# Attention and an exact-GELU feed-forward layer on one core: the first batch's masks, loads and order rewritten

## The chip, the core and the metric

The kernel runs on one core of a Trainium2 chip. A core has TensorE (PE, matmuls into PSUM), VectorE (DVE), ScalarE (ACT), GpSimd (POOL) and SyncE (SP), each with its own instruction stream, and 16 DMA engines that serve the queues of all of them. The metric is the device time of one execution in microseconds (us); lower is better. Before the change the median of 10 runs was 339.84 us (338.58 to 342.14).

## What is computed

Eight batches of eight heads of causal attention over 576 positions of 64 dimensions, with a decay bias from a running sum of s, and then a feed-forward layer over the 4608 tokens (512 to 2048 to 512) with the exact GELU.

```python
scores = scale * np.matmul(q, k.transpose(0, 1, 3, 2))
cum = np.cumsum(np.maximum(s, 0.0), axis=-1)
bias = -(cum[:, :, :, None] - cum[:, :, None, :])
scores = np.where(causal, -1000000000.0, scores + np.minimum(bias, 0.0))
attn = softmax(scores)
x = np.matmul(attn, v)            # to (tokens, heads * dims)
h = x @ w_in
out = (0.5 * h * (1.0 + erf(h / sqrt(2)))) @ w_out
```

The kernel uses that the bias splits into a factor per key position, exp(cum), that can be multiplied into v and into the denominator; numbers that would not allow it send it into a general branch at its end, which these inputs do not take.

## The kernel before

The work goes in chunks of 512 tokens, nine in all; chunk c is the feed-forward work on tokens whose attention was done beforehand, and the attention of batch b = c + 1 is placed between the matmuls of chunk c by a table written by hand. Batch 0 has no chunk to hide in: it is a prologue. The instructions of each engine stand in the order in which the code is written.

A batch's attention has these steps, each a function. `load_qk(b, i, g)` (line 85) loads q (i = 0) or k (i = 1) of one group g of four heads by four DMAs on GpSimd's queue that cast fp32 to bf16 on the way; `load_v` and `load_w` load v (fp32), w_in (`which` 0) and w_out (1), the weights in four pieces each, cast as well. `tr_qk` (197) transposes q or k of a group on VectorE. `sc_item` (348) computes the scores of one group and one unit: unit 0 covers the first two key blocks of 128, unit 1 the other three; four heads take 32 rows of the array each and run beside one another, and ScalarE takes the exp of two heads at a time into P. `mk_item` (359) multiplies the diagonal blocks of P by a 0/1 triangle on VectorE. `weights` (234) makes the running sum `cum` on VectorE, transposes it on TensorE and takes its exp on ScalarE into `wb`; `scale_v` multiplies v by it, `den_col` puts it beside v as a 65th column. `av_item` (422) multiplies P with that for one block `it` of 128 queries; VectorE then takes the reciprocal and scales. `to_xT` (402) transposes the result for the feed-forward layer, by TensorE and a VectorE copy, or by DMA. `absmax` and `square_v` feed a check of ranges.

Chunk c then has layer 1, `l1_item` (449), w_in times xT and the GELU on ScalarE, eight items of two row blocks; and layer 2, `l2_item` (469), which sums 16 matmuls for each block of 128 tokens in one PSUM buffer of two, and evicts it (in chunk 0 by ScalarE) to `o_sb`. `groups` runs layer 2 in steps and calls what the table `side` has for each step. In chunk 0 layer 1 runs twice over 256 tokens, so that it can begin when two blocks of batch 0 are there; `late` names the rest of batch 0's AV between its items.

The prologue has functions of its own. `sc_first` (372) computes scores two heads at a time. It does not use `mk_item`: two more matmuls per piece (line 393) add -30000 above the diagonal by a product of the identity (`ident_bf`) and a mask (`neg_bf`), which `masks` (192) makes on VectorE. k of both groups comes as fp32 into `k0_st`, group 0 on ScalarE's queue, group 1 on SyncE's behind s, and ScalarE casts each (`cast_k0`, 136); q comes through GpSimd. `filler(n)` (416) runs n matmuls of zeros on TensorE, whose results nobody reads. The order is written from line 505 on: the table load for exp, the cast of group 0, 16 fillers, `weights`, the cast of group 1, 4 fillers, all of GpSimd's loads, and then the transposes, scores and AV.

GpSimd's queue before the change: q of group 0, the two triangular selects that make `ident` and `uptri`, q of group 1, v and w_in mixed, two pieces of w_out, q and k of batch 1's group 0, a piece of w_out, q, a piece of w_out, k, v of batch 1.

Of the kernel before, what the change touches and what calls it, by code (L numbers as in the profile page):

```python
# [19 lines left out]
def kernel(  # L20
# [10 lines left out]
    nc = tc.nc  # L31
    fp32 = mybir.dt.float32
# [89 lines left out]
    k0_st = work.tile([128, HG, S * 2], fp32, tag="rawv", bufs=2, name="k0_st")  # L122

    def load_k0(g, eng):

        for h in range(4):
            eng.dma_start(
                out=k0_st[h * 32 : h * 32 + 32, g, :].rearrange("p (t c) -> p t c", c=2 * D),
                in_=bass.AP(
                    tensor=k.tensor,  # L130
                    offset=k.offset + (4 * g + h) * S * D,
                    ap=[[2 * D, 32], [64 * D, SB], [1, 2 * D]],
                ),
            )

    def cast_k0(g):
        nc.scalar.activation(raws[0, "qk"][:, 1, g, :], k0_st[:, g, :], func=AF.Copy)
# [3 lines left out]
    load_k0(0, nc.scalar)  # L141
    load_k0(1, nc.sync)
# [15 lines left out]
    nc.vector.memset(zero, 0.0)  # L158
    ident = const.tile([128, 128], fp32, name="ident")
# [8 lines left out]
    load_qk(0, 0, 1)  # L168
# [21 lines left out]
    neg_bf = const.tile([128, 128], bf16, name="neg_bf")  # L190
# [43 lines left out]
    def weights():  # L234
# [3 lines left out]
        nc.vector.tensor_scalar(cum, s_pos, s_pos[:, 287:288], None, op0=ALU.subtract)  # L238
        t_ps = ps.tile([128, ST, BH], fp32, tag="av", bufs=2, name="t_ps")
# [132 lines left out]
    def sc_first(g, u):  # L372

        if u == 0:
            P_of[0, g] = work.tile([128, 4, PW], bf16, tag="P", bufs=2, name="P")
# [3 lines left out]
        for h2 in range(2):  # L379
            s_ps = ps.tile([128, 2, 512], fp32, tag="sc", bufs=2, name="sc_ps")  # L380
            for jt, i0, n, off in UNITS[u]:
                for e in range(2):
                    for h in range(2):
# [5 lines left out]
                            start=(e == 0), stop=False, tile_position=(h0, 0),  # L389
                        )  # L390
                m = min(n, 128)
                for h in range(2):
                    nc.tensor.matmul(  # L393
                        s_ps[:, h, off : off + m], lhsT=ident_bf, rhs=neg_bf[:, :m],
                        start=False, stop=True,
                    )
# [109 lines left out]
    cast_k0(0)  # L506
    filler(16)
    weights()
    cast_k0(1)
    filler(4)  # L510
# [31 lines left out]
    filler(2)  # L542
    to_xT(0, 0, True)
    filler(1)
    to_xT(0, 1, True)
    gelu_set()
# [7 lines left out]
    for c in range(NCH):  # L554
# [4 lines left out]
        if c == 0:  # L559

            late = [
                [(scale_v, 0, 2), (av, 0, 0, 2)], [(av, 0, 1, 2)],
                [(scale_v, 0, 3), (av, 0, 0, 3)], [(av, 0, 1, 3), (to_xT, 0, 2, True)],
                [(scale_v, 0, 4), (av, 0, 0, 4)], [(av, 0, 1, 4), (to_xT, 0, 3, True)],
                [], [(to_xT, 0, 4, True)],
            ]
            for half in range(2):
                for f2 in range(FT // 2):
                    l1_item(0, f2, half * 256, half * 256 + 256)
                    for f, *a in late[f2] if half == 0 else []:  # L570
                        f(*a)
            for g in range(HG):
                absmax(0, g)
# [21 lines left out]
        if b < B:  # L595
# [5 lines left out]
            if c == 0:  # L601
                for st in range(3):
                    square_v(0, st)
                side = [[] for _ in range(16)]
                side[3] = [(sc, b, 0, 0)]
                side[5] = [(sc, b, 0, 1), (mk, b, 0, 0), (square_v, 0, 3), (square_v, 0, 4)]
                side[6] = [(tr_qk, b, 0, 1), (tr_qk, b, 1, 1)]
                side[9] = [(mk, b, 0, 1), (scale_v, b, 0)]
                side[10] = [(sc, b, 1, 0), (scale_v, b, 1)]
                side[11] = [(av, b, 0, 0), (scale_v, b, 2)]  # L610
                side[12] = [(av, b, 0, 1), (sc, b, 1, 1), (mk, b, 1, 0), (av, b, 0, 2), (scale_v, b, 3)]
                side[13] = [(av, b, 1, 0), (av, b, 0, 3), (scale_v, b, 4)]
                side[14] = [(av, b, 1, 1), (mk, b, 1, 1)]
                side[15] = [
                    (av, b, 1, 2, True), (av, b, 1, 3, True), (to_xT, b, 2, True), (to_xT, b, 3, True)
                ]
# [8 lines left out]
            else:  # L625

                side = [[] for _ in range(16)]
                sc_at = (2, 5, 7, 10) if b < 4 else (2, 5, 8, 11)
# [5 lines left out]
                for at, (g, u) in zip((5, 8, 11, 13 if b < 4 else 14), [(0, 0), (1, 0), (0, 1), (1, 1)]):  # L634
                    side[at].append((mk, b, g, u))
# [165 lines left out]
```

## Time and profile before

| | |
|---|---|
| median of 10 runs | 339.84 us |
| the profiled execution, its own time | 340.57 us |
| its span, first to last instruction | 338.8 us |
| TensorE busy, mean granted clock | 318.6 us (94%), 0.959 |
| VectorE, ScalarE, GpSimd busy | 189.3, 187.5, 87.2 us |
| prologue: to the first layer-1 matmul | 35.20 us, granted clock 0.66 |
| layer 1 of chunk 0 | 35.20 to 52.67 us |
| layer 2 of chunk 0 with batch 1's attention | to 76.7 us |

In the tables of the profile a busy time is the time in which an engine had an instruction under way, and "x" counts instructions. In the timeline the columns are the start, the length, the engine, the line of the kernel, the operation, what it writes and reads, and in brackets the idle time of that engine just before and what ended it. "PEclk" is the share of its full clock that TensorE was granted. A DMA's row gives what it carries, the queue that issued it, the number of issues and the time from issue to landing.

### The profile page before, as it was taken

To read this page: it belongs to the slowest core of one execution; us is meant where nothing else is said; L and a number is where in the kernel's file an instruction comes from. 1 tells how busy PE (TensorE), PEld (TensorE's weight loads), DVE (VectorE), ACT (ScalarE), POOL (GpSimd) and SP (SyncE) were. 2 spreads that over 40 slices of the span, in tenths; PEclk is the share of its full clock that TensorE was granted. 3 is DMA by queue.
4 is the path that set the end of the run, shared out by engine and by line. 5 is a ranking of instruction groups with operands and counts; after the bars stand their busy time and mean duration, and the time that the engine had idled before them with its cause. 6 is when DMAs were issued, how large, how long until landed. Compare 5 with 4: busy or idle time off the path is not lost.

```text
span 338.8 us, 6343 instructions
## 1 busy us (share of the span) xinstructions
PE 318.6 (94%) x2549; PEld 158.4 (47%) x2549; DVE 189.3 (56%) x393; ACT 187.5 (55%) x249; POOL 87.2 (26%) x144
## 2 busy tenths in 40 slices
PE   7599899789998999899999999999999999999992
PEld 2135785344444544454445444545454545444440
DVE  5502672499946794678458744965596542150020
ACT  1445358655877466746576657656857494204400
POOL 7844739103782019000900190000000000000000
PEclk9655999999999999999999999999999999999997
DMA  9999989628999709670998199701310221110011
GB/s 185 218 224 180 152 187 95 111 80 174 139 213 180 185 11 144 123 185 12 134 132 186 26 155 142 172 8 64 93 33 8 77 83 31 41 62 32 3 65 68
DMA packets 92376, 37.35 MB, mean 110 GB/s; under 512 B 80691, under 2 KB 87091, under 8 KB 92339
## 3 DMA queue, kind: packets, MB, share of 16 engines
q0 software_dynamic: 41440, 15.41, 38.6%
q1 hardware_dynamic: 49680, 20.87, 25.5%
q10 hardware_dynamic: 1216, 0.59, 0.7%
q8 instruction: 22, 0.36, 0.4%
q14 instruction: 18, 0.12, 0.1%
HBM read 36.85 MB, written 9.44 MB: 137 GB/s over the span
## 4 chain that ended last, share of the span: by engine, by line
PE 87%; DVE 6%; DMA 2%; ACT 1%; issue 1%; POOL 0%; ACTq 0%; DVEq 0%; POOLq 0%
PE h_ps L460 36%; PE o_ps L476 34%; PE av L428 5%; PE sc_ps L340 5%; PE sc_ps L385 3%; DMA raw_qk<-in_q_dram 2%; PE sc_ps L393 2%; DVE x L438 2%; PE f_ps L420 1%; DVE P L363 1%; DVE vv L222 1%; ACT sq L214 1%; PE xt_ps L411 1%; ACT P L355 1%; DVE o_sb L486 1%
## 5 line engine op out<-in xcount | busy, mean ns | idle before, releaser
L476 PE MATMUL o_ps<-w_out_r,gT 128*128 128x512 bf16 x576 | 135.3, 380 | 1.9 <-ACT o_sb L484 1.9
L460 PE MATMUL h_ps<-xT,w_in_r 128*128 128x512 bf16 (+1 forms) x640 | 132.6, 358 | 1.3 <-DVE xT L414 1.0
L465 ACT ACTIVATE gT<-h_ps 128x1024 bf16<-128x1024 f32 (+1 forms) x80 | 74.8, 938 | 73.9 <-PE h_ps L460 73.5
L460 PEld LDWEIGHTS <-w_in_r 128*128 128x128 bf16 x640 | 59.9, 98 | 55.2 <-issue 2.2
L476 PEld LDWEIGHTS <-gT 128*128 128x128 bf16 x576 | 52.1, 98 | 59.6 <-issue 5.2
L355 ACT ACTIVATE P<-sc_ps 128x1024 bf16<-128x1024 f32 x56 | 54.3, 1021 | 35.0 <-PE sc_ps L340 35.0
L91 POOL DMA_DIRECT2D raw_qk<-in_q_dram x64 | 38.6, 616 | 100.8 <-DVE amx L206 76.7
L486 DVE COPY o_sb<-o_ps 128x512 f32<-128x512 f32 x32 | 22.1, 692 | 59.2 <-PE o_ps L476 59.2
L437 DVE RECIPROCAL rc<-av 128x4 f32<-128x4 f32 (+1 forms) x80 | 14.3, 178 | 59.4 <-PE av L428 59.2
L206 DVE TENSOR_REDUCE amx<-raw_qk 128x2 f32<-128x2304 bf16 x16 | 40.2, 2536 | 0.0
L428 PEld LDWEIGHTS <-P 128*128 128x128 bf16 x576 | 28.2, 99 | 20.9 <-DVE P L363 3.9
L91 POOL DMA_DIRECT2D raw_qk<-in_k_dram x56 | 33.7, 620 | 10.7 <-DMA w_out_r<-in_moe_w_out_dram 5.3
L428 PE MATMUL av<-vv,P 128*128 128x65 bf16 x576 | 32.2, 196 | 3.7 <-DVE P L363 2.3
L438 DVE TENSOR_TENSOR x<-av,rc 128x256 bf16<-128x256 f32 (+1 forms) x80 | 33.8, 423 | 2.8
L363 DVE TENSOR_TENSOR P<-P,tri_bf 128x1024 bf16<-128x1024 bf16 x28 | 19.2, 686 | 13.0 <-ACT P L355 13.0
L222 DVE TENSOR_TENSOR vv<-raw_v,wb 128x512 bf16<-128x512 f32 (+1 forms) x40 | 25.8, 688 | 0.0
L199 DVE STREAM_TRANSPOSE qkT<-raw_qk 128x576 f32<-128x576 f32 x32 | 23.0, 754 | 3.8 <-DMA raw_qk<-in_q_dram 3.8
L214 ACT ACTIVATE sq<-raw_v 128x512 bf16<-128x512 f32 (+1 forms) x40 | 24.6, 624 | 0.0
L340 PE MATMUL sc_ps<-qkT 32*128 32x256 bf16 (+2 forms) x560 | 18.3, 250 | 0.0
L340 PEld LDWEIGHTS <-qkT 32*128 32x128 bf16 x560 | 11.8, 92 | 12.3 <-issue 11.2
L398 ACT ACTIVATE P<-sc_ps 128x1024 bf16<-128x1024 f32 x8 | 8.2, 1023 | 12.7 <-PE sc_ps L393 12.7
L385 PE MATMUL sc_ps<-qkT 32*128 32x256 bf16 (+2 forms) x80 | 10.4, 357 | 4.2 <-DVE qkT L199 4.2
(75 smaller groups left out, 109.7 us busy)
## 6 DMA issues: line engine op xcount, KB each, us to landing
out_dram<-o_sb SPq DMA_DIRECT2D x36, 256.0 KB, 2.4
raw_v<-in_v_dram SPq DMA_DIRECT2D x24, 256.0 KB, 4.0
raw_qk<-in_q_dram POOLq DMA_DIRECT2D x64, 72.0 KB, 3.9
raw_qk<-in_k_dram POOLq DMA_DIRECT2D x56, 72.0 KB, 4.1
raw_v<-in_v_dram POOLq DMA_DIRECT2D x8, 256.0 KB, 5.5
w_in_r<-in_moe_w_in_dram POOLq DMA_DIRECT2D x4, 512.0 KB, 9.2
w_out_r<-in_moe_w_out_dram POOLq DMA_DIRECT2D x4, 512.0 KB, 11.1
raw_v<-in_v_dram SPq DMA_DIRECT2D x6, 128.0 KB, 4.2
```

The lines of the kernel that those rows point to most:

```text
L91: nc.gpsimd.dma_start(out=raws[b, "qk"][h * 32 : h * 32 + 32, i, g, :].rearrange("p (t c) -> p t c", c=2 * D), in_=bass.AP(tensor=src.tens ...
L206: nc.vector.tensor_reduce(amx[:, b * HG + g], raws[b, "qk"][:, :, g, :], axis=AX, op=ALU.max, apply_absolute_value=True,)
L214: nc.scalar.activation(sq[:n_st], raws[b, "v"][:n_st, st].rearrange("p h d -> p (h d)"), func=AF.Square, accum_out=sumv[:n_st, b, st : st ...
L222: nc.vector.tensor_tensor(vv[b % 2][:n_st, st, :, 0:D], raws[b, "v"][:n_st, st, :, :], w.unsqueeze(2).to_broadcast([n_st, H, D]), op=MULT,)
L340: nc.tensor.matmul(s_ps[h // 2][:, h % 2, off : off + n], lhsT=qk[r, 1, g, jt * 128 : jt * 128 + 128, e], rhs=qk[r, 0, g, i0 : i0 + n, e], ...
L355: nc.scalar.activation(P[:, 2 * h2 : 2 * h2 + 2, o : o + 512], s_ps[h2], func=AF.Exp, scale=scale)
L428: nc.tensor.matmul(o_ps[:, h, :], lhsT=P[:, h, off : off + 128], rhs=vv[b % 2][:, jt, 4 * g + h, :], start=(i == 0), stop=(i == len(BLK[it ...
L438: nc.vector.tensor_tensor(x_of[b, it][:n, g * 256 : g * 256 + 256].rearrange("p (h d) -> p h d", d=D), o_ps[:n, :, 0:D], rc[:n].unsqueeze( ...
L460: nc.tensor.matmul(h_ps[:, i, :], lhsT=w_in_r[:, ko, ft * 128 : (ft + 1) * 128], rhs=xT[:, ko, c * NB + n0 : c * NB + n1], start=(ko == 0) ...
L465: nc.scalar.activation(gT_of[c][:, f2 * 2 : f2 * 2 + 2, n0:n1], h_ps, func=AF.Gelu)
L476: nc.tensor.matmul(y_of[c, sub], lhsT=gT[:, ft, sub * 128 : (sub + 1) * 128], rhs=w_out_r[:, ft, :], start=(ft == 0), stop=(ft == FT - 1),)
L486: nc.vector.tensor_copy(o_sb, y_of[c, sub])
```

## The change

Batch 0's masks move from TensorE to VectorE: `sc_first` loses the mask matmuls, and `mk_item` is called for batch 0 too. k of group 0 alone comes as fp32, on SyncE's queue behind s, and is cast in two halves, one by ScalarE and one by VectorE; q and k of group 1 both come through GpSimd, issued right behind q of group 0 and ahead of the selects for `ident` and `uptri`. TensorE gets 26 fillers in a row at the start. `weights` splits: its running sum stays early (`cum_sum`), its transposes and exps come after the first scores. The loads of w_out go ahead of all of batch 1. The prologue interleaves scores, products, AV and transposes in a new order; `late` places batch 0's remaining AV over both halves of layer 1, with three of its squares. In chunk 0's layer 2 each block of 128 tokens runs by itself, where before the first two ran as a pair, with a new table `side`; and in later batches up to 3 the last unit's scores and products come one step earlier.

```diff
-    def load_k0(g, eng):
+    def load_k0(eng):
...
-    def cast_k0(g):
-        nc.scalar.activation(raws[0, "qk"][:, 1, g, :], k0_st[:, g, :], func=AF.Copy)
+    def cast_k0():
+        nc.scalar.activation(raws[0, "qk"][:, 1, 0, :S], k0_st[:, :S], func=AF.Copy)
+        nc.vector.tensor_copy(raws[0, "qk"][:, 1, 0, S:], k0_st[:, S:])
...
-    load_k0(0, nc.scalar)
-    load_k0(1, nc.sync)
+    load_k0(nc.sync)
     load_qk(0, 0, 0)
...
     nc.vector.memset(zero, 0.0)
+    load_qk(0, 0, 1)
+    load_qk(0, 1, 1)
     ident = const.tile([128, 128], fp32, name="ident")
...
-    load_qk(0, 0, 1)
...
     def masks():
-        nc.vector.tensor_scalar(neg_bf, uptri, 30000.0, -30000.0, op0=MULT, op1=ALU.add)
...
-                            start=(e == 0), stop=False, tile_position=(h0, 0),
+                            start=(e == 0), stop=(e == 1), tile_position=(h0, 0),
                         )
-                m = min(n, 128)
-                for h in range(2):
-                    nc.tensor.matmul(
-                        s_ps[:, h, off : off + m], lhsT=ident_bf, rhs=neg_bf[:, :m],
-                        start=False, stop=True,
-                    )
             filler(1)
...
     exp_set()
-    cast_k0(0)
-    filler(16)
-    weights()
-    cast_k0(1)
-    filler(4)
+    filler(26)
...
-    load_w(1, 0)
-    load_w(1, 1)
-    for i in range(2):
-        load_qk(1, i, 0)
-    for i in range(2):
-        load_w(1, 2 + i)
-        load_qk(1, i, 1)
+    for i in range(4):
+        load_w(1, i)
+    load_qks(1)
     load_v(1, nc.gpsimd)
+    cum_sum()
+    cast_k0()
     tr_qk(0, 0, 0)
-    masks()
     tr_qk(0, 1, 0)
     sc_first(0, 0)
-    sc_first(0, 1)
-    den_col(0)
+    weights()
+    filler(2)
     tr_qk(0, 0, 1)
     tr_qk(0, 1, 1)
+    masks()
     sc_first(1, 0)
+    mk_item(0, 0, 0)
+    den_col(0)
     for st in range(2):
         scale_v(0, st)
+    sc_first(0, 1)
     av_item(0, 0, 0)
+    mk_item(0, 1, 0)
+    av_item(0, 1, 0)
+    sc_first(1, 1, (0,))
     av_item(0, 0, 1)
-    sc_first(1, 1)
-    av_item(0, 1, 0)
+    sc_first(1, 1, (1,))
+    to_xT(0, 0, True)
     av_item(0, 1, 1)
     filler(2)
-    to_xT(0, 0, True)
-    filler(1)
     to_xT(0, 1, True)
+    mk_item(0, 0, 1)
+    scale_v(0, 2)
+    mk_item(0, 1, 1)
     gelu_set()
...
-                side[3] = [(sc, b, 0, 0)]
+                side[4] = [(sc, b, 0, 0)]
...
-                groups(c, (0, 1), side[:8])
-                groups(c, (2,), side[8:12])
-                groups(c, (3,), side[12:])
+                for sub in range(4):
+                    groups(c, (sub,), side[4 * sub : 4 * sub + 4])
...
-                sc_at = (2, 5, 7, 10) if b < 4 else (2, 5, 8, 11)
+                sc_at = (2, 5, 7, 9) if b < 4 else (2, 5, 8, 11)
```

On TensorE, at the end of the first half unit of scores (`sc_ps` is the score buffer, `qkT` the transposed q and k, `f_ps<-zero` a filler), before:

```order
L385 LDWEIGHTS qkT_105
L385 MATMUL sc_ps<-qkT_105 128x256
L393 LDWEIGHTS ident_bf
L393 MATMUL sc_ps<-neg_bf,ident_bf 128x128
L393 LDWEIGHTS ident_bf
L393 MATMUL sc_ps<-neg_bf,ident_bf 128x128
L420 LDWEIGHTS zero
L420 MATMUL f_ps<-zero 128x512
L385 LDWEIGHTS qkT_105
L385 MATMUL sc_ps<-qkT_105 128x256
```

The same place after:

```order
L385 LDWEIGHTS qkT_105
L385 MATMUL sc_ps<-qkT_105 128x256
L414 LDWEIGHTS zero
L414 MATMUL f_ps<-zero 128x512
L385 LDWEIGHTS qkT_105
L385 MATMUL sc_ps<-qkT_105 128x256
```

The two mask matmuls and their weight loads are gone from each piece; score, filler and the next half follow one another.

On VectorE, from the running sum of s to the products of batch 0, before:

```order
L238 TENSOR_SCALAR cum<-s_pos 64x576
L199 STREAM_TRANSPOSE qkT_105<-raw_qk 128x9x2x32
L193 TENSOR_SCALAR neg_bf<-uptri 128x128
L194 CAST ident_bf<-ident 128x128
L195 CAST tri_bf<-uptri 128x128
L199 STREAM_TRANSPOSE qkT_105<-raw_qk 128x9x2x32
L230 COPY vv_103<-wb 128x40
L199 STREAM_TRANSPOSE qkT_105<-raw_qk 128x9x2x32 x2
L222 TENSOR_TENSOR vv_103<-raw_v,wb 128x8x64 x2
```

The same stretch after (`k_st` is the fp32 k, `P` the exps, `tri_bf` the 0/1 triangle):

```order
L236 TENSOR_SCALAR cum<-s_pos 64x576
L138 CAST raw_qk<-k_st 128x576
L197 STREAM_TRANSPOSE qkT_105<-raw_qk 128x9x2x32 x4
L192 CAST ident_bf<-ident 128x128
L193 CAST tri_bf<-uptri 128x128
L363 TENSOR_TENSOR P<-P,tri_bf 128x4x2x128
L228 COPY vv_103<-wb 128x40
L220 TENSOR_TENSOR vv_103<-raw_v,wb 128x8x64 x2
L431 RECIPROCAL rc<-av 128x4
L432 TENSOR_TENSOR x<-av,rc 128x256
L363 TENSOR_TENSOR P<-P,tri_bf 128x4x2x128
```

Half of k's cast stands ahead of the transposes, the masks' operations behind all four of them, and the products of P stand between the work for AV.

On GpSimd, the loads from the last two pieces of w_in on (`raw_qk` here is batch 1's), before:

```order
L155 DMA w_in_r<-in_moe_w_in_dram 128x4x512 x2
L155 DMA w_out_r<-in_moe_w_out_dram 128x4x512 x2
L91 DMA raw_qk<-in_q_dram 32x9x128 x4
L91 DMA raw_qk<-in_k_dram 32x9x128 x4
L155 DMA w_out_r<-in_moe_w_out_dram 128x4x512
L91 DMA raw_qk<-in_q_dram 32x9x128 x4
L155 DMA w_out_r<-in_moe_w_out_dram 128x4x512
L91 DMA raw_qk<-in_k_dram 32x9x128 x4
L113 DMA raw_v<-in_v_dram 128x8x64 x4
```

The same loads after:

```order
L155 DMA w_in_r<-in_moe_w_in_dram 128x4x512 x2
L155 DMA w_out_r<-in_moe_w_out_dram 128x4x512 x4
L91 DMA raw_qk<-in_q_dram 32x9x128 x4
L91 DMA raw_qk<-in_k_dram 32x9x128 x4
L91 DMA raw_qk<-in_q_dram 32x9x128 x4
L91 DMA raw_qk<-in_k_dram 32x9x128 x4
L113 DMA raw_v<-in_v_dram 128x8x64 x4
```

The four pieces of w_out stand together, and batch 1's q and k follow them, where half of these loads stood between the pieces before.

More of the change, by code (lines that the diff above doesn't have):

```diff
@@ L378, in sc_first @@
         qk = qkT[0]
-        for h2 in range(2):
+        for h2 in halves:
             s_ps = ps.tile([128, 2, 512], fp32, tag="sc", bufs=2, name="sc_ps")
@@ L569 @@
                     l1_item(0, f2, half * 256, half * 256 + 256)
-                    for f, *a in late[f2] if half == 0 else []:
+                    for f, *a in late[8 * half + f2]:
                         f(*a)
+                    if half == 0 and f2 in (3, 5, 7):
+                        square_v(0, f2 // 2 - 1)
             for g in range(HG):
```

45 lines of the change are left out of this document (22 added, 23 removed).

## The prediction

> **What bounds the kernel now.** I read the page first, then the windows by stage, then the timeline of the first 75 us and the DMA answers. From the page, the load on the engines over the span:
>
> ```profile
> PE   7599899789998999899999999999999999999992
> PEclk9655999999999999999999999999999999999997
> DMA  9999989628999709670998199701310221110011
> ```
>
> TensorE is busy almost everywhere, so the end moves with TensorE. Two things stand out near the start: the granted clock is at 0.5 to 0.6 in slices 2 to 4 (each slice is 8.5 us), and the DMA engines are full for 50 us. The windows of the prologue and of chunk 0's layer 1 (columns: length, busy time of each engine, granted clock, DMA share, GB/s), and finer ones around the clock's changes (length, PE busy, clock, DMA):
>
> ```profile
> 0.00:35.20 35.20, 28.60 (x188) 11.17 (x189) 12.83 (x35) 13.34 (x14) 22.20 (x38) 0.66 1.18 196
> 35.20:52.67 17.47, 16.51 (x188) 14.62 (x188) 12.78 (x23) 8.96 (x15) 9.12 (x14) 1.00 0.94 161
> ...
> 8.00:8.50 0.50, 0.31 (x2) 1.00 1.57 209
> 10.50:11.00 0.50, 0.00 (x0) 0.88 1.28 334
> 34.50:35.00 0.50, 0.18 (x2) 0.73 0.45 29
> ```
>
> The prologue costs 35.2 us and almost all of batch 0's scores run at half clock. Matmuls stop at 8.31. A window's mean of 0.88 puts the drop to 0.5 at 10.88; 0.73 puts the return at 34.77. Next, the timeline at the places that set the prologue's length:
>
> ```profile
> 1.21 5.02 PE L420 MATMUL f_ps<-zero 128*128 128x512 bf16 x16 [1.21 <-DVE zero L158]
> 9.03 1.16 ACT L137 ACTIVATE raw_qk<-k_st 128x1152 bf16<-128x1152 f32 x1 [5.06 <-DMA k_st<-in_k_dram]
> 10.10 0.36 ACT L245 ACTIVATE wb<-t_ps 128x256 bf16<-128x256 f32 x1
> 10.53 0.78 DVE L199 STREAM_TRANSPOSE qkT<-raw_qk 128x576 f32<-128x576 f32 x1 [3.83 <-DMA raw_qk<-in_q_dram]
> 11.73 0.77 DVE L199 STREAM_TRANSPOSE qkT<-raw_qk 128x576 f32<-128x576 f32 x1
> 12.55 0.61 PE L385 MATMUL sc_ps<-qkT 32*128 32x256 bf16 x4 [4.24 <-DVE qkT L199]
> 14.71 0.61 PE L385 MATMUL sc_ps<-qkT 32*128 32x256 bf16 x4
> 15.25 0.39 PE L393 MATMUL sc_ps<-neg_bf,ident_bf 128*128 128x128 bf16 x2
> 16.30 0.63 PE L420 MATMUL f_ps<-zero 128*128 128x512 bf16 x1
> 16.55 1.02 ACT L398 ACTIVATE P<-sc_ps 128x1024 bf16<-128x1024 f32 x1 [1.14 <-PE sc_ps L393]
> 16.87 0.61 PE L385 MATMUL sc_ps<-qkT 32*128 32x256 bf16 x4
> 35.20 1.03 PE L460 MATMUL h_ps<-xT,w_in_r 128*128 128x256 bf16 x8 [0.52 <-DVE xT L414]
> ```
>
> q's landing releases the first transpose at 10.53, the scores start at 12.55, and then one half unit takes 2.16 us from 14.71 to 16.87: two pieces of scores at 0.54 (14.71 to 15.25), two pairs of mask matmuls at 0.33 (to 15.58), a filler at 0.43. ScalarE needs 1.02 of that and idles. So up to 35 us the bound is q's landing, then TensorE at half clock.
>
> **The first score.** How the first transfers share the engines, 0 to 20 us, and the landing of the last of SyncE's k transfers (issued 3.22) and of the last q transfer of group 0 (issued 3.2):
>
> ```profile
> q10 hardware_dynamic: 1216, 0.59, 11.1%
> ...
> k_st<-in_k_dram SPq DMA_DIRECT2D x1, 144.0 KB, 6.7
> ...
> raw_qk<-in_q_dram POOLq DMA_DIRECT2D x1, 72.0 KB, 7.2
> ```
>
> k lands at 9.9 on SyncE's queue and q at 10.4. ScalarE's four k transfers take 11.1% of 20 us, 2.2 us of all 16 engines, and they leave this contest: the second group of k comes by GpSimd behind both groups of q. I take k at 7.7 and q at 8.3; they cannot be later than 9.9 and 10.5 unless the second group gets in front, and 6.6 is my lower end for k, if SyncE's queue gains one and a half times what ScalarE's gives up. The cast is halved over two engines, 1.16 / 2 = 0.6, and hidden under q's landing. VectorE then transposes q and k (0.75 each, the rows at 10.53 and 11.73); the masks' three operations no longer stand between. First score: 8.4 + 1.5 = 9.9 in place of 12.55. Of the 26 fillers the first 16 end at 6.2, and ten more at 0.22 at 8.4: TensorE is idle for 1.6 us in place of 4.2.
>
> **The pace of the scores.** Rows at full clock (three timelines: four fillers; four heads' scores and the exps; AV, VectorE's share of it, the mask product, and a gap in layer 2):
>
> ```profile
> 7.27 1.04 PE L420 MATMUL f_ps<-zero 128*128 128x512 bf16 x4
> 37.19 0.41 PE L428 MATMUL av<-vv,P 128*128 128x65 bf16 x8
> 37.63 0.18 DVE L437 RECIPROCAL rc<-av 128x4 f32<-128x4 f32 x1 [0.47 <-PE av L428]
> 37.84 0.42 DVE L438 TENSOR_TENSOR x<-av,rc 128x256 bf16<-128x256 f32 x1
> 56.22 0.63 PE L340 MATMUL sc_ps<-qkT 32*128 32x256 bf16 x16
> 56.89 1.94 ACT L355 ACTIVATE P<-sc_ps 128x1024 bf16<-128x1024 f32 x2 [0.16 <-PE sc_ps L340]
> 61.51 0.69 DVE L363 TENSOR_TENSOR P<-P,tri_bf 128x1024 bf16<-128x1024 bf16 x1 [0.61 <-ACT P L355]
> 62.12 0.28 DVE L368 TENSOR_TENSOR P<-P,tri_bf 128x256 bf16<-128x256 bf16 x1
> 63.22 2.75 PE L476 MATMUL o_ps<-w_out_r,gT 128*128 128x512 bf16 x12 [1.88 <-ACT o_sb L484]
> 34.72 0.42 DVE L414 COPY xT<-xt_ps 128x512 bf16<-128x512 bf16 x1 [0.43 <-PE xt_ps L411]
> ```
>
> The change takes 40 mask matmuls off TensorE. A half of unit 0 at full clock: scores between 0.54 (half of 1.08) and 0.63, plus a filler 0.22: about 0.86; unit 1 has 2.5 pieces, 1.0. An exp takes 0.97. ScalarE becomes the bound for six exps and the 0.5 to 0.6 of wb's two exps between them (0.36 for the larger): the first exp starts at 10.7, with 0.05 to 0.1 of handover the sixth ends at 17.3. Then comes what the masks cost on VectorE: AV of the first block (16.4), its 0.6 on VectorE, the second product (17.35 to 18.0), AV 0.2, scores 0.8; exp seven starts at 19.2. After it AV 0.43 and scores 0.8, exp eight 20.7. Beside exp eight run the transposes, the last AV (21.0 to 21.5), two fillers, VectorE's 0.6, transposes, and the copy 0.42: layer 1 starts at 23.3. The products of unit 1 (0.97 each) and scale_v stand behind that copy on VectorE and end at 25.6; who waits for them is AV of blocks 2 to 4, which the change has set one layer-1 item later. Gain at this point: 35.2 - 23.3 = 11.9 us, of which 2.6 come from the earlier first score. Ends: 22.5 with k at 6.6, 25.5 with q at 10.5.
>
> **Does the clock stay?** This decides most of the sum. It fell 2.57 us after the last matmul, and came back 23.89 us later. The hole of 1.88 us before 63.22 left it whole (the windows show 1.00 there). I compare stretches of 3.4 us, a seventh of 23.89. In the one that ended with the fall, 7.48 to 10.88, TensorE was busy for 0.83 us; in one that kept the clock, 62.1 to 65.5, for 2.3. In the changed prologue the thinnest, 15.7 to 19.1, holds 1.8 by the steps above: between the two, nearer to the one that kept it. Against it stands the old prologue, which had matmuls without a gap from 12.55 and was not given the full clock back for 22 us, so 32-row scores may count for little. I keep the full clock as the likelier and 11.9 for the sum, and price the other below.
>
> [...]
>
> **Layer 1 and layer 2 of chunk 0.** Weight landings and the two gaps on TensorE that the change addresses (waits of TensorE over the whole span):
>
> ```profile
> w_in_r<-in_moe_w_in_dram POOLq DMA_DIRECT2D x1, 512.0 KB, 11.6
> ...
> w_out_r<-in_moe_w_out_dram POOLq DMA_DIRECT2D x1, 512.0 KB, 13.5
> ...
> w_out_r<-in_moe_w_out_dram POOLq DMA_DIRECT2D x1, 512.0 KB, 14.3
> ...
> 31.69 0.60 POOL L91 DMA_DIRECT2D raw_qk<-in_k_dram  x1 [1.96 <-DMA w_out_r<-in_moe_w_out_dram]
> ...
> PE av L428 <- DVE P L363: 2.3, 5, 0.5
> PE o_ps L476 <- ACT o_sb L484: 1.9, 1, 1.9
> PE av L428 <- DVE vv L222: 1.4, 3, 0.5
> ```
>
> The last w_in piece, issued at 14.7, lands at 26.3; w_out pieces issued at 15.39 and 17.11 land at 28.9 and 31.4, 2.5 apart. GpSimd now issues its first 12 transfers before the identity and the triangle (8.7), and v a little later; the engines are full either way, so I leave w_in at 26.5. Layer 1 uses the last piece at its seventh item, about 30. Loaded in a row, w_out ends at 31.4 + 5.0 = 36.4, batch 1's first q and k group at 40 (before, 34.8 - 31.4 = 3.4 us after w_out), the second at 45, v at 50 (GpSimd issues each q or k in 0.60, v in somewhat more). Layer 1 lasts 17.47 less two of the vv waits (0.9): it ends at 39.9, and w_out is there. Scores of batch 1 come after 20 layer-2 matmuls, 4.3 us, at 44.2: k has landed and been transposed by 42. The second group is wanted near 49, v near 49 to 52. Covers of 1 to 4 us, thin but positive; if they are gone, each us late is a us of TensorE.
>
> In layer 2 one block at a time replaces two: the 1.9 us wait for o_sb goes, since each block's accumulator is copied while the next runs; the third vv wait (0.4) and the first P wait (0.5) go too, two fillers add 0.4: 2.4 less. In batches 2 and 3 the last product moves one step of 0.86 us ahead of an AV that waited 0.45, four times: 1.8 at best, 0 at worst, 1.0 taken. The remaining chunks keep their work.
>
> Sum: 11.9 + 0.9 + 2.4 + 1.0 = 16.2. The profiled execution took 340.57 (span 338.8 and 1.8 around it), 0.7 above the median of 339.84. 340.57 - 16.2 = 324.4, or 323.6 from the median; I forecast 324.
>
> **Rivals.** (1) The clock falls partway, near 16: the last 7 us of prologue hold 4 us of matmuls that double in part, and layer 1 starts slow for up to 3.4 us: layer 1 at 26 and 1.7 lost, 4.4 in all: 328. (2) It falls at the start, because q lands as late as before or because 32-row scores count for little: halves take 1.5 to 1.8, layer 1 starts at 30.2 (scores at 9.9) to 32.3 (scores at 12): 340.6 - 5.0 - 4.3 = 331 to 333. For it: the 22 us at half clock; against: the bridged gap. (3) Slower: batch 1's q and k now wait behind all weights, and TensorE stands idle in layer 2 for them. Before, its first scores came at 56.21 with 48 layer-2 matmuls left, after with 44, so the change loses from a first score at 57 on, k landing near 55; I reckon 40. Were GpSimd's queue to add 17 us, the time would be 342. Against it: the same bytes had all landed by 49 before.
>
> **How the numbers follow.** The forecast has 0.58, rival 1 0.17, rival 2 0.21, rival 3 0.03, and 0.01 that the parts cancel. Range: below, 22.5 for layer 1 and all gaps gone, 321; above, rival 2's first end, 332. A measurement of this kernel can tell about 0.5% (1.7 us) from no change. Forecast and rivals 1 and 2 are all faster by more than that: 0.95 with a little of rival 2 taken off; same 0.02, slower 0.03.
>
> **What would show it.** First scores near 10; a granted clock of 1.00 in every window from 4 to 40; ScalarE's exps back to back from 10.7 to 17; layer 1 near 23, layer 2 near 40; no wait for o_sb and none for raw_qk in layer 2. A clock of 0.5 in 14 to 24 is rival 1 or 2. A wait of TensorE for qkT in layer 2 would make my DMA reckoning wrong.

## The result, and the profile after

The changed kernel took 323.99 us in the median of 9 runs (322.82 to 328.27), the old one 339.54 us in 31 runs beside it: a ratio of 0.9545, with a 95% interval of 0.9513 to 0.9577. The forecast was 324.0. The profiled execution, which is not one of the nine, took 326.84 us (span 325.0), longer than most, and that matters below.

The load over the span, after:

```profile
span 325.0 us, 6288 instructions
...
PE   8888999899999999999999999999999999999992
...
PEclk9759999999999999999999999999999999999998
DMA  9999999989997199629962897212111331010011
```

The low clock fills less than two slices (of 8.1 us) where it filled nearly three (of 8.5). The prologue in finer stages (length, busy time of PE, PEld, DVE, ACT and POOL, granted clock, DMA share, GB/s):

```profile
8.00:10.00 2.00, 1.02 (x8) 0.39 (x8) 1.93 (x4) 0.57 (x1) 1.91 (x5) 1.00 1.61 157
10.00:12.00 2.00, 2.00 (x23) 1.03 (x17) 1.10 (x2) 1.57 (x2) 2.00 (x3) 0.93 0.79 105
12.00:14.00 2.00, 2.00 (x12) 0.54 (x10) 1.90 (x6) 0.74 (x3) 2.00 (x4) 0.50 0.75 190
...
22.00:24.00 2.00, 2.00 (x28) 1.33 (x22) 0.61 (x2) 1.02 (x1) 0.68 (x1) 0.50 1.23 211
24.00:26.00 2.00, 2.00 (x21) 1.33 (x17) 0.88 (x3) 1.88 (x2) 1.28 (x3) 0.66 1.24 206
```

So in this execution the clock fell after all, at 11.7 in place of 10.9, and came back at 25.4 in place of 34.8. The places of the timeline that answer to those of before:

```profile
7.88 0.68 ACT L137 ACTIVATE raw_qk<-k_st 128x576 bf16<-128x576 f32 x1 [5.85 <-DMA k_st<-in_k_dram]
7.90 0.46 DVE L138 CAST raw_qk<-k_st 128x576 bf16<-128x576 f32 x1 [1.64 <-DMA k_st<-in_k_dram]
8.28 2.28 DVE L197 STREAM_TRANSPOSE qkT<-raw_qk 128x576 f32<-128x576 f32 x3
9.77 0.63 PE L385 MATMUL sc_ps<-qkT 32*128 32x256 bf16 x8 [0.98 <-DVE qkT L197]
10.32 0.39 PE L414 MATMUL f_ps<-zero 128*128 128x512 bf16 x1
10.64 0.63 PE L385 MATMUL sc_ps<-qkT 32*128 32x256 bf16 x8
14.61 1.03 PE L385 MATMUL sc_ps<-qkT 32*128 32x256 bf16 x8
15.58 0.61 PE L414 MATMUL f_ps<-zero 128*128 128x512 bf16 x1
16.12 1.04 PE L385 MATMUL sc_ps<-qkT 32*128 32x256 bf16 x12
20.75 0.40 PE L422 MATMUL av<-vv,P 128*128 128x65 bf16 x4 [1.33 <-DVE P L363]
27.01 1.91 PE L454 MATMUL h_ps<-xT,w_in_r 128*128 128x256 bf16 x16 [0.51 <-DVE xT L408]
43.79 4.48 PE L470 MATMUL o_ps<-w_out_r,gT 128*128 128x512 bf16 x20
```

k lands at 7.9 (9.0 before), q is there when VectorE's half of the cast ends, and the first score stands at 9.77 in place of 12.55. At full clock a half unit takes 0.87 us (9.77 to 10.64), at half clock 1.50 (14.61 to 16.12), where it took 2.16 with the mask matmuls. The new wait for the product on VectorE is there: 1.33 us at 20.75. Layer 1 starts at 27.01 in place of 35.20, layer 2 at 43.79 in place of 52.67. What TensorE waits for over the whole span (us, times, longest):

```profile
PE av L422 <- DVE P L363: 1.8, 2, 1.3
PE f_ps L414 <- DVE zero L158: 1.2, 1, 1.2
PE h_ps L454 <- DVE xT L408: 1.0, 2, 0.5
PE sc_ps L385 <- DVE qkT L197: 1.0, 1, 1.0
PE av L422 <- DVE vv L220: 0.9, 3, 0.4
```

The 1.9 us for `o_sb` is gone, and so are the four waits for P in batches 2 and 3. Taken along the chain of chunk starts, the 13.8 us between the two spans are: 8.2 at the start of layer 1, 0.7 in layer 1 (16.8 in place of 17.5), 1.8 in layer 2 of chunk 0 (22.3 in place of 24.0), 2.5 in chunks 1 and 2 (33.6 to 32.4 and 34.2 to 32.9), 0.6 in the rest.

The executions differ in how much of them ran at full clock. Mean granted clock and span of all eleven (the nine and two more, of which the profiled one, at 0.975, alone has a trace):

| clock | 0.967 | 0.972 | 0.975 | 0.979 | 0.991 | 0.991 | 0.994 | 0.996 | 0.998 | 0.998 | 0.998 |
|---|---|---|---|---|---|---|---|---|---|---|---|
| span | 326.4 | 326.4 | 325.0 | 325.4 | 322.1 | 322.2 | 321.0 | 323.3 | 321.5 | 321.8 | 322.2 |

Seven are near 322 and four near 326; the ratio leaves out the two slowest as a slower state, though they only lie at the end of this same row. The 13.7 us at half clock of the profiled execution make the difference between 0.998 and 0.975, so 3.41 us of it, a quarter, and the length of the one loss in the run with the pair below (19.43 to 22.84), take 0.005 to 0.006 off the mean.

### The profile page after: what moved, and what is told of

Same layout as the page of the kernel before. It is cut to its first block, busy times and chain, and to the rows that moved or that the text cites. A ratio compares the mean times of both kernels' runs of the same rounds, so it can differ in the third digit from the quotient of the medians.

```text
span 325.0 us, 6288 instructions
## 1 busy us (share of the span) xinstructions
PE 312.1 (96%) x2518; PEld 158.6 (49%) x2518; DVE 192.5 (59%) x399; ACT 185.8 (57%) x248; POOL 89.8 (28%) x148
## 4 chain that ended last, share of the span: by engine, by line
PE 92%; DVE 4%; DMA 1%; issue 1%; POOL 1%; DVEq 0%; POOLq 0%
PE h_ps L454 38%; PE o_ps L470 38%; PE av L422 5%; PE sc_ps L340 5%; PE sc_ps L385 2%; PE f_ps L414 2%; DMA raw_qk<-in_q_dram 1%; DVE x L432 1%; PE xt_ps L405 1%; DVE vv L220 1%; POOL raw_qk L91 1%; DVE P L363 1%; DVE rc L431 0%; DVE xT L408 0%; DVE qkT L197 0%
## 5 line engine op out<-in xcount | busy, mean ns | idle before, releaser
L91 POOL DMA_DIRECT2D raw_qk<-in_k_dram x60 | 36.3, 622 | 10.0 <-DMA w_out_r<-in_moe_w_out_dram 8.0
L422 PE MATMUL av<-vv,P 128*128 128x65 bf16 x576 | 31.4, 196 | 2.7 <-DVE P L363 1.8
L363 DVE TENSOR_TENSOR P<-P,tri_bf 128x1024 bf16<-128x1024 bf16 x32 | 22.0, 686 | 10.5 <-ACT P L355 10.4
L340 PE MATMUL sc_ps<-qkT 32*128 32x256 bf16 (+2 forms) x560 | 18.4, 250 | 0.0
L340 PEld LDWEIGHTS <-qkT 32*128 32x128 bf16 x560 | 12.0, 92 | 12.7 <-issue 11.6
L414 PE MATMUL f_ps<-zero 128*128 128x512 bf16 x40 | 14.3, 481 | 1.2 <-DVE zero L158 1.2
## 6 DMA issues: line engine op xcount, KB each, us to landing
w_in_r<-in_moe_w_in_dram POOLq DMA_DIRECT2D x4, 512.0 KB, 10.5
```

The lines of the kernel that those rows point to most:

```text
L91: nc.gpsimd.dma_start(out=raws[b, "qk"][h * 32 : h * 32 + 32, i, g, :].rearrange("p (t c) -> p t c", c=2 * D), in_=bass.AP(tensor=src.tens ...
L340: nc.tensor.matmul(s_ps[h // 2][:, h % 2, off : off + n], lhsT=qk[r, 1, g, jt * 128 : jt * 128 + 128, e], rhs=qk[r, 0, g, i0 : i0 + n, e], ...
L363: nc.vector.tensor_tensor(d, d, tri_bf.unsqueeze(1).unsqueeze(1).to_broadcast([128, 4, 2, 128]), op=MULT)
L422: nc.tensor.matmul(o_ps[:, h, :], lhsT=P[:, h, off : off + 128], rhs=vv[b % 2][:, jt, 4 * g + h, :], start=(i == 0), stop=(i == len(BLK[it ...
```

## The experiments

All start from the changed kernel. Each was timed in five rounds beside the old kernel, except the last, which ran once. They ran in three batches of four, on three chips; the old kernel's median beside them was 339.58, 339.58 and 338.94 us. The theory: the gain is the shorter prologue, and its clock decides how short. The rival: the clock is immaterial, and what counts is the matmuls that left TensorE.

**Fewer fillers.**

```diff
-    filler(26)
+    filler(16)
```

> The changed kernel with 16 fillers at the start in place of 26, nothing else. Theory (the granted clock decides the prologue): matmuls stop near 6.3 us and the scores start near 9.8, so the clock falls in every run near 8.5 or 11.9 at the latest; layer 1 starts at 27 to 29.5 us, time 326.5 to 329.5 us, granted clock 0.96 to 0.975, no run under 326. Rival (ScalarE and VectorE bound the new prologue and the clock is immaterial): 324 us with the same spread as the changed kernel.

Measured: 327.85 us (327.18 to 328.85), all six executions with a clock of 0.963 to 0.975. Layer 1 started at 27.2. The theory holds, the rival does not: ten matmuls on zeros, taken away, cost 4 us against the median of the changed kernel, and nothing against those of its executions that lost the clock. Two stretches of this run, each 3.41 us long, the second ending where the clock fell (length, PE busy, clock, DMA share, GB/s):

```profile
4.68:8.09 3.41, 1.85 (x9) 1.00 1.50 196
8.09:11.51 3.42, 1.88 (x20) 1.00 1.32 133
```

Both are 54 to 55% busy. The first, all fillers, was followed by full clock; the second, mostly scores of 32 rows, by half clock. In the profiled execution of the changed kernel the stretch that ended with the fall was even 71% busy:

```profile
8.29:11.71 3.42, 2.44 (x24) 1.00 1.22 129
```

**More fillers.** `filler(31)` at the start, and five in the wait:

```diff
     av_item(0, 0, 0)
+    filler(5)
     mk_item(0, 1, 0)
```

> The changed kernel with 31 fillers at the start and five more in the 1.3 us wait between the two first AV items. Theory: TensorE has no hole before the first score and a smaller one later, fewer runs lose the clock, 322.5 to 323.8 us, layer 1 near 23.5. Rival (the clock is immaterial): 324 us or 0.1 to 0.3 more for fillers that the scores wait for. If scores of 32 rows count too little, part of the runs still fall to 0.97 and 327.

Measured: 324.50 us (323.70 to 326.47), clocks of 0.992 to 0.998 in all six, so none can have had much more than one stretch of 3.41 us at half clock. In the profiled execution the prologue kept its clock, and layer 1 started at 22.45, 0.9 before the forecast's 23.3. But the time is that of the changed kernel, as the rival has it. The profiled execution is the longest of the six (the others are at 323.70 to 324.92); it shows where its lead went:

```profile
22.45 1.91 PE L454 MATMUL h_ps<-xT,w_in_r 128*128 128x256 bf16 x16 [0.51 <-DVE xT L408]
...
44.73 0.63 PE L340 MATMUL sc_ps<-qkT 32*128 32x256 bf16 x16 [0.94 <-DVE qkT L197]
...
63.66 3.50 PE L454 MATMUL h_ps<-xT,w_in_r 128*128 128x512 bf16 x8 [1.62 <-DMA xT<-x]
```

Layer 1 is 4.6 us ahead of the profiled execution above, and layer 2 4.5 us; then TensorE waits 0.94 us for batch 1's k, and chunk 1 waits 1.62 us for the DMA transposes of batch 1's first blocks. Chunk 1 starts only 2.4 us ahead. Its first eight matmuls take 3.50 us where they take 1.89 undisturbed, for the clock fell behind the wait, at 63.8:

```profile
62.00:64.00 2.00, 0.38 (x3) 0.16 (x3) 1.92 (x2) 0.00 (x0) 0.00 (x0) 0.94 1.47 254
64.00:66.00 2.00, 2.00 (x6) 0.73 (x5) 2.00 (x2) 0.00 (x0) 0.00 (x0) 0.50 1.37 269
```

So this execution, whose prologue was the shorter, ended with a span of 324.7.

**Two fillers behind each half unit**, with the 31 and the five.

> As the run with 31 fillers, and two fillers behind each half unit of scores in place of one. Theory: no window is thin enough, every run has a clock of 0.99 or more, 322.5 to 324.0 us, layer 1 at 23.3 to 24.3 since the second filler just about fills the time that ScalarE needs for an exp. Rival (clock immaterial): up to 1 us slower than the changed kernel, since eight fillers of 0.22 are added to TensorE's row.

Measured: 325.31 us (324.51 to 326.99); clocks of 0.989 to 0.998. Layer 1 started at 24.1, 1.7 later than with one, more than ScalarE hides. By the medians the second filler costs 0.8 us, which the rival had, and it buys nothing that the 31 had not bought.

**k as before**, both groups as fp32 on two hardware queues, cast whole by ScalarE, and 43 fillers.

> The changed kernel with k loaded and cast as before (both groups as fp32, on ScalarE's and SyncE's queues, whole casts on ScalarE), and 43 fillers at the start so that TensorE is busy until about 12. Theory: the first score goes back to about 12.3, 2.5 us later, and layer 1 with it: 326 to 327 us, clock as in the changed kernel. Rival (the start is covered: loads or VectorE bound layer 1 anyway): 324 us.

Measured: 325.53 us (325.41 to 325.96). The first score stood at 13.49, but not for the reason meant: k landed at 8.4, q at 9.6, both transposes of group 0 were done at 11.0, and the 43 fillers held TensorE. The run doesn't price the loads of k; it prices the start. Against the run with 31 fillers the first score is 3.3 us later, layer 1 3.3 us later (25.7), and the time 1.0 us longer: two thirds were given back, and in the two traces what differs on the way is that here neither batch 1's k nor the DMA transposes are waited for. By these ends the first score could have stood near 11.0 with k as before, an estimate. The five fillers in the wait are not in this run, which waits 1.33 us for the product, and its clocks are 0.988 to 0.995 all the same.

**The old order of w_out and batch 1's q and k.**

```diff
-    for i in range(4):
-        load_w(1, i)
-    load_qks(1)
+    load_w(1, 0)
+    load_w(1, 1)
+    for i in range(2):
+        load_qk(1, i, 0)
+    for i in range(2):
+        load_w(1, 2 + i)
+        load_qk(1, i, 1)
```

> The changed kernel with w_out and batch 1's q and k loaded in the old order. Theory: the last piece of w_out lands at 43 to 44 in place of 39, and layer 2 of chunk 0, which wants it 2.6 us after its start at 40 to 44, waits 0 to 2 us on TensorE; the other loads are early: 324 to 325.5 us. Rival (the order of the loads carries the gain): layer 2 stands still for 4 us or more, 328 us. Second rival (q and k being late is the new bound): 322 to 323 us.

Measured: 328.07 us (327.06 to 328.43). The theory's size was wrong, the first rival's 328 us right. The profiled execution had lost its clock (0.968, layer 1 at 27.6) and shows no wait for w_out, while four others at 0.983 to 0.986 were as slow. The last run below has this order at full clock.

**Masks as matmuls again**, `masks` ahead of the first scores, and no `mk_item` for batch 0.

```diff
-                            start=(e == 0), stop=(e == 1), tile_position=(h0, 0),
+                            start=(e == 0), stop=False, tile_position=(h0, 0),
                         )
+                m = min(n, 128)
+                for h in range(2):
+                    nc.tensor.matmul(
+                        s_ps[:, h, off : off + m], lhsT=ident_bf, rhs=neg_bf[:, :m],
+                        start=False, stop=True,
+                    )
...
-    mk_item(0, 0, 0)
...
-    mk_item(0, 1, 0)
...
-    mk_item(0, 0, 1)
     scale_v(0, 2)
-    mk_item(0, 1, 1)
```

> The changed kernel with batch 0's masks as matmuls again: 40 mask matmuls back on TensorE, no products on VectorE for batch 0. Theory: at full clock 40 x 0.08 = 3 to 4 us of matmuls go into a stage that ScalarE bounds by then, so half of it shows, against 1.3 us of VectorE's chain that goes; 324 to 326 us, and the clock keeps better, since these matmuls use all rows. Rival (the move of the masks is the main gain): 328 us or more.

The edit also puts the loads of group 1's q and k behind the two selects, and `masks` between the first two transposes.

Measured: 332.50 us in the median of six. Two executions at a clock of 0.994 took 325.94 and 326.11 us, as the theory has it; four at 0.963 to 0.967 took 332.45 to 333.56, as the rival has it. Against the changed kernel's executions of like clock, and with all of the edit put down to the masks, they are worth 2 us at full clock (span 324.2 against 321.0 to 323.3) and 4.4 at a clock of 0.967 (330.8 against 326.4). That these matmuls would hold the clock was wrong: it fell at 12.0 in the profiled execution. The masks' three operations on VectorE stand ahead of k's transpose here (in the old kernel they take 0.5 us between two transposes, 11.23 to 11.73), and the first score stands at 9.96.

**The first two blocks of layer 2 as a pair again.**

```diff
-                for sub in range(4):
-                    groups(c, (sub,), side[4 * sub : 4 * sub + 4])
+                groups(c, (0, 1), side[:8])
+                groups(c, (2,), side[8:12])
+                groups(c, (3,), side[12:])
```

> The changed kernel with the first two blocks of chunk 0's layer 2 as a pair again, the new table of side items kept. Theory: both accumulators are full until 32 matmuls are done, the third block waits for ScalarE's copy as before (1.9 us), and the side items come after other matmuls: 325 to 326.5 us. Rival (the wait was covered): 324 us.

Measured: 325.81 us (324.52 to 330.30). Two of the six, at clocks of 0.970 and 0.971, took 329.71 and 330.30; the others 324.52 to 326.04. The wait is back:

```profile
50.02 1.89 PE L470 MATMUL o_ps<-w_out_r,gT 128*128 128x512 bf16 x8 [1.54 <-ACT o_sb L478]
```

So the term is real, 1.5 of the 1.9. The times alone would not show it: the ratio to the old kernel, 0.9576 (0.9535 to 0.9617), can't be told from 0.9545. This run also has a prologue, unchanged in its code, that kept its clock until 19.4, in two stretches of 77% and 99%, and lost it after the third, of 61%, in which AV waits for the product:

```profile
9.19:12.60 3.41, 2.63 (x25) 1.00 1.07 159
12.60:16.01 3.41, 3.37 (x44) 1.00 1.02 170
16.01:19.43 3.42, 2.09 (x38) 1.00 1.18 227
19.43:22.84 3.41, 2.75 (x28) 0.50 1.16 244
```

Layer 1 starts at 23.03. And chunk 1 waits longer for the DMA transposes than with 31 fillers, but here the clock stays, and its first eight matmuls take 1.89 us:

```profile
65.12 1.89 PE L454 MATMUL h_ps<-xT,w_in_r 128*128 128x512 bf16 x8 [1.89 <-DMA xT<-x]
```

**The later batches' last unit at its old steps**, `sc_at` with 10 for 9, and the products at 11 and 13 again.

> The changed kernel with the last unit's scores and products of batches 2 and 3 at their old steps. Theory: four waits of 0.45 us come back, 325 to 325.8 us. Rival: they are hidden, 324 us.

Measured: 328.23 us (326.35 to 331.09), more than expected. The waits for P come back:

```profile
PE av L422 <- DVE P L363: 3.7, 6, 1.3
```

Layer 2 of chunks 1 and 2 lasts 19.4 us each in place of 18.1, so 2.5 us in all, of which the four waits are 1.9. The rest of the 4.2 us between the medians stays open: the profiled execution also waited 2.1 us for the DMA transposes and lost the clock for 3.4 us each in the prologue (from 19.8 on) and in chunk 1 (from 64.2 on), and the other five have no trace.

**Batch 1's first blocks transposed by TensorE.**

```diff
-                side[12] = [(av, b, 1, 0), (av, b, 0, 2), (scale_v, b, 3)]
-                side[13] = [(av, b, 1, 1), (av, b, 0, 3), (mk, b, 1, 1)]
-                side[14] = [(scale_v, b, 4)]
+                side[12] = [(av, b, 1, 0, True), (av, b, 0, 2), (scale_v, b, 3)]
+                side[13] = [(av, b, 1, 1, True), (av, b, 0, 3), (to_xT, b, 0, True), (mk, b, 1, 1)]
+                side[14] = [(scale_v, b, 4), (to_xT, b, 1, True)]
```

> The changed kernel with batch 1's first two blocks transposed by TensorE and VectorE in place of the DMA transposes. Theory (where the prologue keeps its clock, layer 1 of chunk 1 waits 0.9 to 2.1 us for these DMA transposes, which share the engines with batch 2's loads): that wait goes, TensorE gets 0.5 us more work, 322 to 323.3 us, the fast executions near 321.5. Rival (the lead is held back further up, by batch 1's k and v): 324 us, the wait only changes its name.

Measured: 324.50 us (322.99 to 328.69), with clocks from 0.971 to 0.998: no gain by itself. The profiled execution had lost the clock, at 11.1, and shows nothing of the wait.

**The same, with 31 fillers and five in the wait.**

> The same with 31 fillers at the start and five in the AV wait. Theory: all executions keep the clock and none waits for the DMA transposes: 321.5 to 323 us, spread under 2 us. Rival: 324 us, as the run with 31 fillers alone.

Measured: 323.42 us (322.93 to 324.57), clocks of 0.996 to 0.999. Its start, and that of chunk 1:

```profile
10.03 0.63 PE L385 MATMUL sc_ps<-qkT 32*128 32x256 bf16 x8
...
22.26 1.91 PE L454 MATMUL h_ps<-xT,w_in_r 128*128 128x256 bf16 x16 [0.52 <-DVE xT L408]
...
62.19 1.89 PE L454 MATMUL h_ps<-xT,w_in_r 128*128 128x512 bf16 x8 [0.52 <-DVE xT L408]
```

Chunk 1 starts 1.5 us earlier than with the fillers alone, at full clock, and the wait for the DMA transposes is gone. So is the wait of 0.94 us for batch 1's k, and that is not the edit's doing: the scores that read it run at 43.45 here, where k landed only at 43.9 there. The ratio to the old kernel, 0.9539 (0.9511 to 0.9566), can't be told from the changed kernel's 0.9545. What differs is the spread, 1.6 us in place of 5.4: no execution is at 327 or 328. In all runs with 31 fillers or more, 31 executions, no clock is under 0.988; in the changed kernel and its four variants with 26 fillers and without mask matmuls it is 0.979 or less in 12 of 36.

**Batch 1's first q and k ahead of the last piece of w_out**, on top of that.

> As the run before, with q and k of batch 1's group 0 loaded ahead of the last piece of w_out. If the loads bind the start of layer 2 (k landed at 43.9 and the scores waited 0.9 us for it in the run with 31 fillers), that wait goes, but the last piece of w_out comes 3 us later than it did and layer 2 wants it 2.6 us after its start: 0 to 1 us slower than the run before. If w_out had slack: 0.5 to 0.9 us faster.

Measured: 326.16 us (325.10 to 327.77), 2.7 us slower than the run before, more than expected. Now w_out is late, which is 1.0 of it; another 0.8 in the profiled execution is its fillers, which ran at the slow pace for longer (first score at 10.82 in place of 10.03, see below), and the rest stays open:

```profile
43.55 1.89 PE L470 MATMUL o_ps<-w_out_r,gT 128*128 128x512 bf16 x8 [0.98 <-DMA w_out_r<-in_moe_w_out_dram]
```

**The old order of the loads at full clock**, one execution, with 31 fillers and five in the wait.

> The changed kernel with the old order of w_out and batch 1's q and k, 31 fillers and five in the AV wait, one look at full clock. Theory: layer 2 of chunk 0 starts near 39.5 and stands still 3 to 5 us for the last pieces of w_out; 326 us. Rival: it doesn't wait for w_out, and the 328 us of that order came from the lost clock alone; 323 us.

Measured: 328.26 us. Layer 1 starts at 22.8, layer 2 at 39.6, and then:

```profile
46.38 2.54 PE L470 MATMUL o_ps<-w_out_r,gT 128*128 128x512 bf16 x8 [3.89 <-DMA w_out_r<-in_moe_w_out_dram]
```

The wait is 3.9 us, and the clock falls behind it (0.50 from 47.5 to 50.9). The prologue that is 12 us shorter (22.8 for 35.20) is worth here what the loads that follow it allow: with the old order the end is the same 328 us whether the clock is kept (328.26) or lost (328.05 in the profiled execution of the other run).

## Why the prediction was right, step by step

The time, the direction and the likeliest mechanism were right, but errors of the sum cancel and the profiled execution shows a rival. That the median meets the forecast to a tenth of a us is luck, with 5.4 us between the shortest and the longest execution.

- **First score.** 9.9 forecast, 9.77 measured, k at 7.9 (7.7). Right. The 2.8 us were not taken apart cleanly. With the old loads of k the transposes end at 11.0, which puts 1.3 of them down to those loads, since both q and k then come later; the masks' operations are 0.5 by the old kernel's rows (11.23 to 11.73); the rest is q, which landed at 9.6 with the old loads of k and at 10.5 in the old kernel, and why is not shown.
- **Pace and the start of layer 1.** Forecast 23.3 at full clock. No execution of the changed kernel that kept it has a trace; the same prologue in the runs with the pair and with the old late steps, which lost it for 3.4 us at its end, starts layer 1 at 23.0 and 22.7, and with 31 fillers and five in the wait at 22.3 to 23.0. The 0.86 per half unit (0.87) and the wait for the product (1.33 measured) were right.
- **The clock.** By the mean clock, seven of the eleven executions kept it but for about one stretch of 3.41 us at most, and four lost it for longer. These four lie at rival 1's time, 328 forecast, 326.8 to 328.3 measured, but the one with a trace did not go rival 1's way: there the clock falls near 16 and layer 1 starts slowly, while here it fell at 11.7, before most of the scores, the half units took 1.50 us as rival 2 has them, and layer 1 started at 27.0 instead of 26 and then ran undisturbed in 16.8. That the time agrees is luck. My ground for a kept clock was not right either. The rows of the old kernel show the 23.89 us at half clock and not the 3.4 of my stretches; the runs showed that length (3.41 us at half clock with the pair, and 13.65, four times that, in the changed kernel). I took TensorE's busy time in a stretch as the measure and put the bound between 0.83 and 2.3 us; the fall came after 2.44, 2.09 and 1.88 us of mixed scores and fillers, while 1.85 us of fillers alone kept the clock.
- **Why one execution keeps the clock and another does not.** The traces of the five kernels with 26 fillers and without mask matmuls, whose code is the same up to the first score on TensorE, give an answer. All start with fillers 0.43 us apart, and at a moment that differs from run to run the pace doubles to 0.22 (the clock column says 1.00 for both). The later that moment, the later the 26 fillers end (8.5 to 9.4), and the smaller is the gap before the first score, which moves less (9.8 to 10.0):

| run | pace doubles at | gap before the first score | TensorE busy in the stretch with the gap, or most of it | clock |
|---|---|---|---|---|
| batch 1's first blocks by TensorE | 4.2 | 1.43 | 58% | falls at 11.1 |
| old order of w_out | 5.0 | 1.21 | 65% | falls at 11.8 |
| the changed kernel | 4.9 | 0.98 | 71% | falls at 11.7 |
| pair | 5.8 | 0.67 | 77% | stays to 19.4 |
| old late steps | 6.2 | 0.43 | 88% | stays to 19.8 |

With 31 fillers or more the traces have no gap there, and none loses the clock before layer 1. The prediction had the 26 fillers end at 8.4. In the profiled execution they ended at 8.8, and that this end moves from run to run is a thing it did not reckon with.

- **Rival 2 was overpriced.** With 16 fillers the clock is low in all six executions; in the profiled one it is lost at 11.5, when two of the eight half units are done, and back at 28.6. Layer 1 starts at 27.2 (30.2 forecast), and the median is 327.85 (331).
- **Loads.** I had w_out landing at 36.4 and batch 1's k at 40, with covers of 1 to 4 us. The last piece of w_out was issued at 23.3 and landed 16.1 later, at 39.4; k landed at 42.6 (issued 39.7, 2.9 to landing). In one of the traces whose layer 2 starts before 40 the cover of k was gone (0.94 us, with 31 fillers); in the others of the new order it held. I had priced this ("each us late is a us of TensorE"), not counted it.
- **What the sum left out.** The DMA transposes of batch 1's first blocks: 0.95, 1.6, 1.9 and 2.1 us of wait in four runs that came to them early, and in two of these 1.7 more at half clock behind it. That batch 2's loads are what slows them was not tested; with 31 fillers GpSimd issued q and k between 56.0 and 61.1, and SyncE the transposes at 56.7 and 58.4. This is rival 3's kind of wait, small: it gave back part of the lead, not all.
- **Layers.** 0.9 forecast for layer 1, 0.7 measured; 2.4 for layer 2, 1.8 measured where it did not wait for loads. The wait for o_sb went as forecast. The two others that the prediction had going did not: AV still waits 0.47 us for P and 0.27 and 0.20 for vv there, where it waited 0.48 and 0.39.
- **Later batches.** 1.0 forecast, 2.5 measured: I took about half of a term (1.8) that came whole, and four waits of 0.45 were not all that the old order cost there.

The sum for an execution with the clock kept would have been 11.9 + 0.9 (layer 1 at 22.4) + 0.7 + 1.8 + 2.5 = 17.8, less up to 0.9 for k and up to 3.2 for the transposes and the clock behind them: 13.7 to 17.8. The seven spans of 321.0 to 323.3 (338.8 less 15.5 to 17.8) lie in its upper half. The forecast's 16.2 lies inside it too: it gave layer 1's start and the later batches 2.4 too little, layer 1 and layer 2 0.8 too much, and the waits behind them nothing. The lower end of the range, 321, does not follow from its terms: 12.7 + 0.9 + 2.4 + 1.8 off 339.84 gives 322.0.

Two things of the change were not tested by themselves: the new order of the prologue's AV, products and transposes, and the new places of batch 0's remaining AV in layer 1.

## What to carry to other kernels

When a stage ahead of a saturated one is shortened, list what the saturated stage will then ask for earlier, with landing times, and take the loads' order into the same change: here the shorter prologue was worth 4 us less with the old order (328.07 against 323.99). A gap of about a us on TensorE (0.98 in the profiled execution) went here with about four lost through the clock, in part of the executions (spans near 326 for 322); fillers in the gaps cost no more than 0.5 us in the median (324.50 against 323.99, with five more at the start and five in the wait), and their benefit shows in the spread over executions (2.8 us in place of 5.4), not only in one profile. Where fillers are counted out to end at a certain time, ask whether their pace is the same in every execution: here it went from 0.43 to 0.22 us at 4.2 to 6.2. Judge such a change from many executions: the one that was profiled here was neither typical nor the worst.

## What the runs showed of the hardware

- The times at half clock come in stretches of 3.41 us: 3.4 in four runs (with the pair, 19.43 to 22.84; with the old late steps, 19.80 to 23.22; with 31 fillers, from 63.8; in the last run, from 47.5), 13.65 in the changed kernel (11.71 to 25.36), 17.1 in two runs (16 fillers, 11.51 to 28.57; the old order of w_out, 11.78 to 28.84), 20.5 with mask matmuls (12.00 to 32.48) and 23.89 in the old kernel (10.88 to 34.77) are 1, 4, 5, 6 and 7 of them, and in the run with the old late steps two falls, at 19.80 and 64.2, are 13 of them apart. Counted back from the fall, a stretch also ends where the first fillers double their pace (4.88 in the changed kernel, 5.77 in the run with the pair; by the fillers' own pace 4.9 and 5.8). Where the stretches begin differs from run to run (the falls near the first scores lie at 11.51, 11.71, 11.78 and 12.00).
- The clock fell after stretches in which TensorE was 55 to 71% busy by its rows, with matmuls of 32 rows in them (71% from 8.29 to 11.71 in the changed kernel), and was kept after one with 77% (9.19 to 12.60 with the pair). With full-size matmuls alone it was kept after 54% (16 fillers, 4.68 to 8.09; and, counted back from the fall of the last run near 47.45, 1.85 of the 3.41 us from 40.6 to 44.0) and fell after 32% (1.08 of the 3.41 us behind them there). So, by these rows, the scores count for less than their time. Mask matmuls of all 128 rows among the scores did not keep it (70% busy, 8.59 to 12.00).
- DMA transposes of batch 1's first blocks took 5.6 to 6.1 us to land in the run with the old late steps, which issued the first at 56.1, 5.1 to 5.7 with 31 fillers (56.7), 4.4 to 5.3 with two fillers behind each half unit (57.4), 3.1 to 4.3 in the changed kernel (60.2) and 2.3 to 2.5 in the old kernel (71.8), where the median of all was 2.4.
- The time behind a wait can count: after 1.6 us without work the clock fell and the first eight matmuls of chunk 1 took 3.50 us in place of 1.89; after 1.9 us at the same place in another run it did not, and they took 1.89. There, counted on from that run's fall at 19.43, the wait was spread over two stretches (60.4 to 63.8 and 63.8 to 67.2), which were 67 and 61% busy; in the first case the stretch that ended with the fall at 63.8 held all of it and was 37% busy.
